# Sparse attention and a feed-forward block in one kernel: leftover blocks of two heads in one slot, another order for the first batch, and the last output tile in two halves

## The chip, the cores and the metric

One Trainium2 chip, of which one core is used. The metric is the time of one execution on the device in microseconds. One more execution was recorded by the hardware profiler; durations and positions below are from that one.

## The reference

Attention over 8 batches, 8 heads, 576 positions and a head dimension of 64, in float32. Heads 0 to 3 see the 32 latest positions ("local"), heads 4 to 7 all earlier positions of the same class modulo 32 ("strided"). The result goes through a feed-forward block with a piecewise gate.

```python
scores = scale * np.matmul(q, k.transpose(0, 1, 3, 2))
mask_local = (rel >= 0) & (rel < stride)
mask_strided = (rel >= 0) & (pos[None, :] % stride == pos[:, None] % stride)
...
attn = np.exp(scores)
attn = attn / (np.sum(attn, axis=-1, keepdims=True) + 1e-09)
...
h = x @ w_in                       # 4608 x 512 by 512 x 2048
g = np.where(pos, h, np.where(neg, 0.0, (h + beta) ** 2 / (4.0 * beta)))
return (g @ w_out).astype(np.float32)
```

## The kernel before

**Attention.** Only blocks that the masks leave are computed: a local head has 18 blocks of 32 queries by 64 keys, a strided head (its positions sorted by class) 11 blocks of 54 by 54. A batch is worked on in four units (`UNITS`): unit 0 has local blocks 0 to 11, unit 1 local blocks 12 to 17, unit 2 strided blocks 0 to 5, unit 3 strided blocks 6 to 10. Two heads make a pair `p`, and `j` is the head within the pair, on partitions 64 j and up. Blocks are stacked on the 128 partitions of a slot: four local ones (`IL`) or two strided ones (`IS`). A unit has `n` slots for each `j`; unit 1 needs 1.5 of them and has 2, unit 3 needs 2.5 and has 3. In `score` (L255) the empty part of the last slot is filled by computing blocks of the same unit a second time (L266).

The steps of a unit, with the letters of the `steps` table (L402): `s` scores on TensorE; `m` mask, a minimum with a mask tile on VectorE out of PSUM, for strided units after a small memset on GpSimd (L291, L297); `x` row maximum on VectorE (L302); `a` subtraction on GpSimd (L306); `e` exponential on ScalarE (L310); `q` row sum on VectorE (L314); `p` plus epsilon on ScalarE (L318); `r` reciprocal on VectorE and product on GpSimd (L322, L323; `w` does the product on VectorE); `f` a transpose of each slot on TensorE (L337); `c` or `d` copies the transposes out of PSUM on ScalarE or VectorE (L349); `v` probabilities times values on TensorE (L368); `h` and `l` write the result as a high and a low float32r part, on ScalarE and VectorE (L395, L399), to the ring `xT`. All float32 matmuls of `s` and `v` appear as two records each in the trace.

**Feed-forward.** The 4608 rows go in 9 chunks `c` of 512, and the 2048 columns of `w_in` in 16 units `f` of 128. For each (c, f): `up` has 12 matmuls of 128x128 by 128x512 (four cuts of the depth by three products of high and low parts, L429) into one of two PSUM buffers "h"; `gate` (L432) has two ScalarE instructions and three on VectorE and ScalarE, the last of which (L446, `gl`) frees that PSUM buffer; `down` (L449), two units later, has 12 matmuls again (L454). Buffer "h" of unit f is that of unit f-2, so `up(0, 2)` waits for `gl` of unit 0. In the last unit `down` copies each of four tiles to one of three SBUF buffers `ob` on ScalarE and stores it by SyncE's queue (L457 to L459).

**Weights.** `w` holds, for each f, a half i=0 (of `w_in`) and a half i=1 (of `w_out`) as raw 64-bit numbers. A half is loaded by SyncE (512 KB) and converted in five steps: `conv_a` on ScalarE, an instruction for the high words (L163) and one for the low words (L166); `conv_b` on VectorE (L171); `conv_c` on GpSimd (L176); `conv_d` on ScalarE (L182); `conv_e` on VectorE (L186). During chunk 0 the halves listed in `halves[f]` are converted in step f: `start_w` issues a, b, c ahead of the gate, `end_w` issues d, e behind it. So in step 0 come halves (0, 1) and (2, 0), in step 1 halves (1, 1) and (3, 0), and so on. Halves (0, 0) and (1, 0) are converted ahead of the loop.

**Order.** The order of instructions on each engine is the order of the program (`manual_schedule`, L478). Ahead of the loop, batch 0 goes through all its steps in an order written out by hand (L491 to L514), among `warm` matmuls on zeros and the conversions of (0, 0) and (1, 0). `up(0, 0)` is split in two calls: the first takes cuts 0 and 1 of the depth (the local heads), the second cuts 2 and 3 (the strided heads) and the products with the low part of the weights. Batches 1 to 7 are spread over the steps f of the loop (`STEPS`, L521): of its four strings the first stands right behind `up`, the second behind `start_w`, the third inside the gate, the fourth behind it. Loads of batch 0, of the first halves and of the queries and keys of batch 1 stand in one row on SyncE (L479 to L490).

## Time and profile before

| | us |
|---|---|
| median of 3 runs (lowest, highest) | 914.03 (913.59, 914.49) |
| the profiled execution's own time | 914.18 |
| span of its profile | 912.4 |

| engine | busy in the span, us |
|---|---|
| TensorE | 899.4 |
| its weight loads (beside the matmuls) | 720.9 |
| ScalarE | 414.4 |
| VectorE | 364.1 |
| GpSimd | 123.1 |

How to read it: PE is TensorE, PEld its weight loads, ACT ScalarE, DVE VectorE, POOL GpSimd, SPq SyncE's queue of transfers. L429 is line 429 of the kernel. A row of the timeline has start, duration, engine, line, operation, tile written <- tiles read, shape, how many in a row, and in brackets the idle time of the engine before it with what ended it. Starts are in microseconds from the start of the span. 914.18 is 1.8 us more than the span; this part lies outside the profile.

### The profile page before, as it was taken

To read this page: it belongs to the slowest core of one execution; us is meant where nothing else is said; L and a number is where in the kernel's file an instruction comes from. 1 tells how busy PE (TensorE), PEld (TensorE's weight loads), DVE (VectorE), ACT (ScalarE), POOL (GpSimd) and SP (SyncE) were. 2 spreads that over 40 slices of the span, in tenths; PEclk is the share of its full clock that TensorE was granted. 3 is DMA by queue.
4 is the path that set the end of the run, shared out by engine and by line. 5 is a ranking of instruction groups with operands and counts; after the bars stand their busy time and mean duration, and the time that the engine had idled before them with its cause. 6 is when DMAs were issued, how large, how long until landed. Compare 5 with 4: busy or idle time off the path is not lost.

```text
span 912.4 us, 17478 instructions
## 1 busy us (share of the span) xinstructions
PE 899.4 (99%) x7550; PEld 720.9 (79%) x7551; DVE 364.1 (40%) x611; ACT 414.4 (45%) x754; POOL 123.1 (13%) x137
## 2 busy tenths in 40 slices
PE   7899999999999999999999999999999999999998
PEld 4688878888788878887888878887888888888886
DVE  6999753423443234323433243334342322222221
ACT  4989744343444444443544344344434343334333
POOL 7464311100211011100210021101110000000000
PEclk9999999999999999999999999999999999999999
DMA  9919131200212021210221021211110010001001
GB/s 353 399 44 311 33 116 62 97 27 10 101 51 70 18 91 47 68 36 1 102 87 33 18 102 36 68 35 42 63 48 1 1 47 1 1 0 47 1 1 46
DMA packets 20381, 61.88 MB, mean 68 GB/s; under 512 B 2256, under 2 KB 2256, under 8 KB 20304
## 3 DMA queue, kind: packets, MB, share of 16 engines
q1 hardware_dynamic: 20304, 60.76, 18.8%
q8 instruction: 59, 0.97, 0.4%
q14 instruction: 18, 0.15, 0.0%
HBM read 51.31 MB, written 9.44 MB: 67 GB/s over the span
## 4 chain that ended last, share of the span: by engine, by line
PE 95%; DMA 2%; DVE 1%; ACT 0%; issue 0%; POOL 0%; SPq 0%; ACTq 0%; DVEq 0%
PE o L454 45%; PE h L429 42%; PE xp L368 3%; PE sc L271 3%; PE tp L337 2%; DMA qk<-in_qk_l 2%; DMA out<-ob 1%; DVE pr L297 0%; DVE st L302 0%; ACT ob L458 0%; DVE st L314 0%; POOL pr L323 0%; DVE w L186 0%; DVE raw L171 0%; DVE h L441 0%
## 5 line engine op out<-in xcount | busy, mean ns | idle before, releaser
L429 PE MATMUL h<-xTh,w 128*128 128x512 f32 x1152 | 381.1, 392 | 1.6 <-DVE gl L446 1.0
L454 PE MATMUL o<-w,gh 128*128 128x512 f32 x1152 | 370.6, 403 | 0.4 <-ACT ob L458 0.4
L429 PEld LDWEIGHTS h<-xTh,w 128*128 128x128 f32 x1152 | 216.3, 188 | 50.8 <-ACT raw L163 1.4
L454 PEld LDWEIGHTS o<-w,gh 128*128 128x128 f32 x1152 | 209.8, 188 | 48.5 <-ACT ob L458 1.8
L438 ACT ACTIVATE u<-h,half 128x512 f32<-128x512 f32 x144 | 99.0, 688 | 315.7 <-PE h L429 313.1
L454 PE MATMUL o<-w,gl 128*128 128x512 f32 x576 | 227.7, 395 | 0.0
L429 PE MATMUL h<-xTl,w 128*128 128x512 f32 x576 | 225.5, 391 | 0.4 <-DVE xTl L399 0.4
L441 DVE SCALAR_TENSOR_TENSOR h<-h,u 128x512 f32<-128x512 f32 x144 | 100.2, 696 | 242.6 <-ACT u L439 242.6
L446 DVE TENSOR_TENSOR gl<-h,gh 128x512 fp32r<-128x512 f32 x144 | 99.5, 691 | 84.5 <-ACT gh L443 77.6
L443 ACT CAST gh<-h 128x512 fp32r<-128x512 f32 x128 | 75.1, 587 | 122.3 <-DVE h L441 122.0
L454 PEld LDWEIGHTS o<-w,gl 128*128 128x128 f32 x576 | 108.3, 188 | 26.0
L429 PEld LDWEIGHTS h<-xTl,w 128*128 128x128 f32 x576 | 108.2, 188 | 25.5 <-DVE xTl L399 1.0
L439 ACT ACTIVATE u<-u 128x512 f32<-128x512 f32 x144 | 91.0, 632 | 4.6
L306 POOL TENSOR_TENSOR pr<-pr,st 128x648 f32<-128x648 f32 (+2 forms) x32 | 40.5, 1268 | 366.5 <-DVE st L302 339.5
L399 DVE TENSOR_TENSOR xTl<-xp,xTh 128x192 fp32r<-128x192 f32 (+7 forms) x74 | 34.8, 522 | 95.3 <-ACT xTh L395 95.3
L323 POOL TENSOR_TENSOR pr<-pr,st 128x648 f32<-128x648 f32 (+2 forms) x32 | 40.5, 1268 | 148.1 <-DVE st L322 141.9
L176 POOL TENSOR_TENSOR raw<-raw 128x512 uint32<-128x512 uint32 (+1 forms) x34 | 34.8, 1037 | 38.8 <-DVE raw L171 13.0
L314 DVE TENSOR_REDUCE st<-pr 128x12 f32<-128x648 f32 (+2 forms) x32 | 26.2, 818 | 33.9 <-ACT pr L310 33.9
L271 PEld LDWEIGHTS sc<-qk 64*32 64x32 f32 (+1 forms) x2048 | 26.6, 116 | 14.5 <-issue 7.8
L368 PEld LDWEIGHTS xp<-pT,v 64*64 64x64 f32 (+2 forms) x1760 | 28.6, 135 | 10.7 <-issue 8.8
L271 PE MATMUL sc<-qk 64*32 64x64 f32 (+1 forms) x2048 | 31.4, 224 | 3.2 <-DMA qk<-in_qk_l 1.4
L368 PE MATMUL xp<-pT,v 64*64 64x32 f32 (+2 forms) x1760 | 32.2, 221 | 0.5 <-ACT pT L349 0.4
(39 smaller groups left out, 351.4 us busy)
## 6 DMA issues: line engine op xcount, KB each, us to landing
raw<-in_w SPq DMA_DIRECT2D x30, 512.0 KB, 9.7
qk<-in_qk_s SPq DMA_DIRECT2D x16, 604.0 KB, 5.7
qk<-in_qk_l SPq DMA_DIRECT2D x16, 576.0 KB, 4.6
out<-ob SPq DMA_DIRECT2D x36, 256.0 KB, 3.5
v<-in_v_l SPq DMA_DIRECT2D x21, 384.0 KB, 3.2
v<-in_v_s SPq DMA_DIRECT2D x7, 384.0 KB, 3.9
v<-in_v_s SPq DMA_DIRECT2D x8, 320.0 KB, 3.1
raw<-in_w SPq DMA_DIRECT2D x4, 256.0 KB, 8.3
```

Source lines behind the costliest of these rows:

```text
L176: nc.gpsimd.tensor_tensor(out=H_, in0=H_, in1=L, op=ALU.add)
L271: nc.tensor.matmul(sc[j][i * Q:(i + 1) * Q, s, p], qk[:, 0, q0:q0 + Q], qk[:, 1, k0:k0 + W], start=True, stop=True)
L306: nc.gpsimd.tensor_tensor(out=pr, in0=pr, in1=st[:, 0].unsqueeze(2).broadcast_to(list(pr.shape)), op=ALU.add)
L323: eng.tensor_tensor(out=pr, in0=pr, in1=st[:, 2].unsqueeze(2).broadcast_to(list(pr.shape)), op=ALU.mult)
L368: nc.tensor.matmul(xp[p][j * D:(j + 1) * D, at:at + R], loaded[b, local, b0 + n][half_, j], pT[half_, j, s, i * Q:i * Q + R], start=True, ...
L429: nc.tensor.matmul(o_ps[c, f], wt[f][:, x, 0, cc * P:(cc + 1) * P], xT[y][:, cc, r0:r0 + CH], start=first and n == 0, stop=last and n == l ...
L438: nc.scalar.activation(u, hp, AF.Relu, bias=half, scale=0.5)
L439: nc.scalar.activation(u, u, AF.Square)
L441: nc.vector.scalar_tensor_tensor(out=hp, in0=hp, scalar=1.0, in1=u, op0=ALU.max, op1=ALU.min)
L443: nc.scalar.copy(gh, hp)
L446: nc.vector.tensor_tensor(out=gl, in0=hp, in1=gh.bitcast(F32), op=ALU.subtract)
L454: nc.tensor.matmul(o_ps[c][t], gs[x][:, t * P:(t + 1) * P], wt[f][:, y, 1, :], start=f == 0 and n == 0, stop=f == NF - 1 and n == 2)
```

## The change

Three edits, and one small one.

1. `slots(u)` gives the number of slots for each `j`: (3, 3), (2, 1), (3, 3), (3, 2). `seat` puts the leftover blocks of j=1 behind those of j=0 in the last slot of j=0: on partitions 64 and up, where a second copy of blocks stood before. `score` runs over blocks and computes each once. `mask` treats full slots on 128 partitions and the shared slot in two instructions of 64 partitions. All that follows has fewer slots: 6 instead of 8 groups in unit 1, 10 instead of 12 in unit 3.
2. The first batch is written as one string for a new helper `begin`. Half (2, 0) is converted in it (A20, L20, B20, C20, D20, E20), and `halves` has it no more. The product of unit 1 goes to VectorE (w1 in place of r1), its copy to VectorE (d1) and that of unit 3 to ScalarE (c3). The first part of `up(0, 0)` (U0) stands ahead of v3, the second (U1) behind l3. There are 8 and 9 warm matmuls in place of 7 and 8.
3. The last output tile is copied in two halves, by VectorE and ScalarE, into a tile of the pool "s" in place of "ob", and stored by two transfers.
4. `h3 l3` of a batch moves from inside the gate to behind it (step 14 of `STEPS`).

The renaming that follows from 1 (`probs` and `flipped` no longer carry `n`) is left out below.

```diff
+    def slots(u):
+        n, rest = divmod(UNITS[u][2], IL if UNITS[u][0] else IS)
+        return n + (rest > 0), n
+
+    def seat(u, n, j):
+        I = IL if UNITS[u][0] else IS
+        s, i = divmod(n, I)
+        return (j, s, i) if s < UNITS[u][2] // I else (0, s, i + j * I // 2)
...
         def score(u, pairs=range(2)):
...
             for p in pairs:
-                for s in range(n):
-                    for i in range(I):
-                        blk = b0 + (s * I + i if s * I + i < nb else s * I + i % (nb - s * I))
...
+                for n in range(nb):
+                    q0 = (b0 + n) * (QL if local else WS)
+                    k0 = max(q0 - ST, 0) if local else q0
+                    for j in range(2):
+                        _, s, i = seat(u, n, j)
+                        qk = loaded[b, p0 + p, "qk"][j * D:(j + 1) * D]
+                        nc.tensor.matmul(sc[j][i * Q:(i + 1) * Q, s, p], qk[:, 0, q0:q0 + Q],
+                                         qk[:, 1, k0:k0 + W], start=True, stop=True)
...
         def mask(u):
...
-            for j in range(2):
-                o = pr[:, j * n * 2:(j + 1) * n * 2].rearrange("p (n h) w -> p n h w", h=2)
-                nc.vector.tensor_tensor(out=o, in0=sc[j], in1=m, op=ALU.min)
+            todo = [(j, slice(0, P), 0, ns[1], j * ns[0]) for j in range(2)]
+            if ns[0] > ns[1]:
+                todo += [(j, slice(j * 64, j * 64 + 64), ns[1], ns[0], ns[1]) for j in range(2)]
+            for j, part, s0, s1, at in todo:
...
+                nc.vector.tensor_tensor(out=o, in0=sc[j][part, s0:s1], in1=m.broadcast_to([o.shape[0], n, 2, W]), op=ALU.min)
...
         def flip(u):
...
-            for j in range(2):
+            for j, n in enumerate(slots(u)):
                 tp = psum(kinds(u, "F", j), [P, n, P], f"tp_{b}_{u}_{j}")
...
         def down(c, f, gs):
...
-                ob = o_p.tile([P, DM], F32, tag="ob", name=f"ob_{c}_{t}")
-                nc.scalar.copy(ob, o_ps[c][t])
-                nc.sync.dma_start(out[c * CH + t * P:c * CH + (t + 1) * P, :], ob)
+                e0 = 0 if (c, t) < (NCH - 1, CH // P - 1) else DM // 2
+                if e0:
+                    last = s_p.tile([P, DM], F32, tag="s", name="ob_last")
+                    nc.vector.tensor_copy(last[:, :e0], o_ps[c][t][:, :e0])
+                    nc.sync.dma_start(out[NT - P:, :e0], last[:, :e0])
+                ob = last[:, e0:] if e0 else o_p.tile([P, DM], F32, tag="ob", name=f"ob_{c}_{t}")
+                nc.scalar.copy(ob, o_ps[c][t][:, e0:])
+                nc.sync.dma_start(out[c * CH + t * P:c * CH + (t + 1) * P, e0:], ob)
...
-    for g in range(2, NF):
+    for g in range(3, NF):
         halves[g - 2].append((g, 0))
+
+    def begin(names):
+        conv = {"A": lambda f, i: conv_a(f, i, (False,)), "L": lambda f, i: conv_a(f, i, (True,)),
+                "B": conv_b, "C": conv_c, "D": conv_d, "E": conv_e}
+        for name in names.split():
+            if name[0] == "U":
+                up(0, 0, name == "U0", name == "U1")
+            elif name[0] == "W":
+                warm("o", int(name[1:]))
+            elif name[0] in conv:
+                conv[name[0]](int(name[1]), int(name[2]))
+            else:
+                first(name)
...
-        warm("o", 7)
-        first("s0 s1 s2 s3")
-        warm("o", 8)
-        first("m0 x0 a0 m1 x1 a1 e0 m2 x2 a2 e1")
-        conv_a(0, 0, (False,))
-        first("q0 p0")
-        conv_a(0, 0, (True,))
-        first("e2 r0 m3 x3 a3 q1 p1 r1 f0 c0 e3 q2 p2")
-        conv_b(0, 0)
-        first("r2")
-        conv_a(1, 0)
-        first("v0 f1 q3 p3 r3")
-        conv_c(0, 0)
-        first("f2 h0 c1 d2 l0 v1 f3 h1 d3 l1 v2")
-        conv_b(1, 0)
-        conv_d(0, 0)
-        conv_c(1, 0)
-        first("h2 v3")
-        conv_e(0, 0)
-        first("l2 h3 l3")
-        up(0, 0, last=False)
-        up(0, 0, first=False)
-        conv_d(1, 0)
-        conv_e(1, 0)
+        begin("""
+            W8 s0 m0 x0 s1 m1 s2 s3 m2 x1 a0 x2 e0 L00 q0 a1 a2 e1 q1 p0 p1 A00 r0 m3 x3 W9 e2 a3 L10 q2 f0
+            w1 c0 p2 r2 e3 B00 q3 A10 v0 f1 p3 L20 h0 f2 r3 d1 A20 d2 v1 f3 C00 h1 D00 c3 v2 l0 l1 B20 U0
+            B10 h2 C10 v3 h3 C20 D10 E00 l2 l3 D20 U1 E20 E10
+        """)
...
-                 14: ("v3", "", "h3 l3", "")}
+                 14: ("v3", "", "", "h3 l3")}
```

## The prediction

> **What bounds the kernel now.** I first read the busy time by stretches (columns: stretch, its length, busy time and count of PE, PEld, DVE, ACT, POOL, then granted clock, DMA share, GB/s):

> ```profile
> 0.00:24.36 24.36, 18.10 (x525) 11.85 (x526) 15.49 (x32) 10.87 (x24) 16.78 (x35) 0.93 0.94 357
> 24.36:35.99 11.63, 9.62 (x43) 6.37 (x37) 9.67 (x16) 10.98 (x20) 4.96 (x5) 1.00 1.02 407
> 35.99:130.00 94.01, 94.01 (x959) 75.85 (x959) 78.08 (x135) 74.82 (x141) 39.91 (x40) 1.00 0.42 151
> 130.00:880.00 750.00, 749.63 (x5913) 604.42 (x5913) 254.60 (x421) 307.46 (x555) 61.45 (x59) 1.00 0.13 44
> 880.00:908.05 28.05, 28.05 (x122) 22.44 (x120) 6.25 (x9) 9.67 (x16) 0.00 (x0) 1.00 0.03 9
> 908.05:912.40 4.35, 0.00 (x1) 0.00 (x0) 0.00 (x0) 0.58 (x1) 0.00 (x0) 0.99 0.50 188
> ```

> From 35.99 to 908.05 PE is busy all but 0.37 us, at full clock. Any matmul that leaves this stretch shortens the run by its own time, any work on other engines costs nothing while they keep up. Three places are left: PE's own work in the middle, the way to 35.99, and the 4.35 us behind the last matmul. The edits touch all three.

> **PE's work in the middle (edit 1).** Rows of batch 1, whose steps run between FFN matmuls:

> ```profile
> 35.99 1.17 PE L271 MATMUL sc<-qk 64*32 64x64 f32 x96
> 42.81 0.86 PE L271 MATMUL sc<-qk 64*32 64x64 f32 x64
> 54.81 0.82 PE L337 MATMUL tp<-ident,pr 128*128 128x128 f32 x6
> 61.11 0.92 PE L271 MATMUL sc<-qk 64*64 64x54 f32 x48
> 74.89 0.60 PE L337 MATMUL tp<-ident,pr 128*128 128x128 f32 x4
> ```

> Unit 1 has 8 blocks times 2 pairs times 2 heads before, 6 after: 8 matmuls or 16 records fewer. A record costs (1.17 - 0.86) / 32 = 0.0097 us, so 0.155 us. Unit 3 goes from 48 to 40 records. Its row has 0.92 us; with the fixed part of unit 0's row (1.17 - 96 x 0.0097 = 0.24) a record costs (0.92 - 0.24) / 48 = 0.0142, so 0.11 us. A transpose costs (0.82 - 0.60) / 2 = 0.11, and units 1 and 3 lose one each: 0.22 us. Together 0.49 us a batch, in 7 batches under the FFN **3.4 us**. Bounds: if the doubled blocks ran wholly in the shadow of the others, only the transposes count, 7 x 0.22 = 1.5; the upper end is 3.7 with 0.0192 (0.92 / 48) for each of unit 3's records, 7 x (0.155 + 0.154 + 0.22).

> The mask pays in instructions: two of unit 1 become four.

> ```profile
> L297 DVE TENSOR_TENSOR pr<-sc,m_loc 128x384 f32<-128x384 f32 x16 | 8.2, 552 | 24.0 <-PE sc L271 24.0
> L297 DVE TENSOR_TENSOR pr<-sc,m_loc 128x256 f32<-128x256 f32 x16 | 6.0, 419 | 6.0 <-PE sc L271 6.0
> L302 DVE TENSOR_REDUCE st<-pr 128x12 f32<-128x768 f32 x8 | 7.6, 953 | 0.3
> L302 DVE TENSOR_REDUCE st<-pr 128x8 f32<-128x512 f32 x8 | 5.5, 687 | 0.3
> ```

> 133 ns go with 128 elements, so one of 128 takes 0.29 and four 1.14 against 0.84: 0.3 us more on DVE. Taking 64 partitions like 128 is my choice, no row shows it; at half price the sum is 0.84 again. The row maximum falls from 512 to 384 elements, by 0.13, and the sum likewise: DVE stands even, ACT and POOL gain. In chunk 0 DVE is busy 78.08 of 94.01 us; there the conversion of (2, 0) is gone as well. At no cost, then; without that cover 0.3 us would stand behind each gate.

> **The way to 35.99 (edit 2).** PE, ACT and DVE in the first batch:

> ```profile
> 15.15 0.87 PE L337 MATMUL tp<-ident,pr 128*128 128x128 f32 x6 [0.21 <-POOL pr L323]
> 16.41 1.98 PE L368 MATMUL xp<-pT,v 64*64 64x32 f32 x96 [0.39 <-ACT pT L349]
> 19.34 0.87 PE L337 MATMUL tp<-ident,pr 128*128 128x128 f32 x6 [0.37 <-POOL pr L323]
> 23.52 0.33 PE L368 MATMUL xp<-pT,v_None 54*64 54x54 f32 x7 [0.83 <-issue]
> 25.74 0.51 PE L429 MATMUL h<-xTh,w 128*128 128x512 f32 x1 [0.18 <-ACT xTh L395]
> 26.66 0.50 PE L429 MATMUL h<-xTl,w 128*128 128x512 f32 x1 [0.42 <-DVE xTl L399]
> 32.39 0.47 PE L429 MATMUL h<-xTh,w 128*128 128x512 f32 x1 [1.00 <-DVE gl L446]
> 33.50 0.73 PE L429 MATMUL h<-xTh,w 128*128 128x512 f32 x2 [0.41 <-DVE w L186]
> 37.09 0.73 PE L454 MATMUL o<-w,gh 128*128 128x512 f32 x2
> ```
> ```profile
> 23.87 2.27 ACT L395 CAST xTh<-xp 128x324 fp32r<-128x324 f32 x4 [1.64 <-PE xp L368]
> 28.73 0.67 ACT L438 ACTIVATE u<-h,half 128x512 f32<-128x512 f32 x1
> ```
> ```profile
> 24.65 2.50 DVE L399 TENSOR_TENSOR xTl<-xp,xTh 128x324 fp32r<-128x324 f32 x4 [0.39 <-ACT xTh L395]
> 31.55 0.69 DVE L446 TENSOR_TENSOR gl<-h,gh 128x512 fp32r<-128x512 f32 x1
> 32.16 1.28 DVE L186 TENSOR_TENSOR w<-raw,w 128x512 fp32r<-128x512 f32 x2
> ```

> I walked the new string queue by queue with these durations (those of smaller tiles scaled as above). (a) Up to f0 nothing is won: q0 stands behind as much DVE work, f0 comes at 15.15 again, and the ninth warm matmul lies ahead of it. (b) c0 now stands behind e2 and the low words of (1, 0) on ACT, and v0 starts about 0.4 later, its bulk near 17.2. (c) From there PE runs f1, f2, v1, f3, v2 in one row, for their inputs come from DVE (r1's product, d1) in time: 1.5 + 0.4 + 0.6 + 0.9 + 0.6 + 1.0 put v2's end at 22.2, against 23.85 (23.52 + 0.33), where PE had waited for POOL (0.37) and for its own instructions (0.83). (d) h2 and h3 on ACT follow c3, and h3 waits for v3, which stands behind U0: end 25.1, against 26.14. l3 ends at 25.9 against 27.15, U1 at 27.2 against 28.6. (e) Behind it ACT has D20 and the two instructions for (0, 1), but not the two for (2, 0): the gate of unit 0 runs at 27.2 in place of 28.73 and `gl` ends at 30.75 in place of 32.24. up(0, 1) is through by then, so up(0, 2) still waits, 0.9 of the 1.00 us; the 0.41 us for the weights of unit 2 is gone, for E20 is done at 26.8. up(0, 2) then ends at 33.6 against 36.0. (f) s0 of batch 1 comes next, and needs its queries and keys:

> ```profile
> L222 SPq DMA_DIRECT2D qk<-in_qk_l x4: 328/400/431, 0.7 to 23.2; - x4
> DMA to landing us min/median/max: 4.1/5.8/10.9
> ```

> The second pair is issued at 23.2 and lands 10.9 later, 34.1. The loads ahead of it keep all DMA engines busy and are not touched, so this stays. The second half of s0 (0.55) ends at 34.6 at the earliest, and the first `down` can start 37.09 - 34.6 = **2.5 us** earlier at most. The same walk over the old order gave 36.8 for 37.09, 0.3 too early; I take **2.2 us**. Low end: a pause for instructions of 0.83 ahead of v2 again, and a POOL product that stops a DVE conversion (0.5), leave 0.9.

> Does the gain last through chunk 0? Unit 5's w_in is ready at 50.27 and PE wants it at 52.21:

> ```profile
> 48.99 1.28 DVE L186 TENSOR_TENSOR w<-raw,w 128x512 fp32r<-128x512 f32 x2
> 52.21 2.76 PE h L429 x12
> ```

> 1.9 us of lead. PE moves by 2.2 and ACT, DVE by 1.5 (e), so 0.7 is used up and 1.2 left. Edit 4 (h3, l3 behind the gate) lies beside down(0, 12), up(0, 15) and down(0, 13), three stretches of 2.8 us before anything reads it: at nothing; without these it would cost l3's 1.2 us once.

> The clock speaks against (c):

> ```profile
> 7.80:11.20 3.40, 1.78 (x93) 1.56 (x95) 3.33 (x7) 0.41 (x1) 1.92 (x2) 1.00 0.99 340
> 11.20:14.60 3.40, 3.18 (x26) 1.27 (x19) 3.05 (x7) 3.02 (x6) 2.94 (x4) 0.50 1.02 405
> 14.60:18.00 3.40, 2.72 (x94) 2.04 (x92) 3.13 (x7) 2.22 (x7) 2.91 (x4) 1.00 1.01 398
> ```

> After 1.78 busy us in 3.40 the granted clock fell to 0.50, after 2.72 it stayed. With v0 later the new stretch has 0.4 of warm matmuls, 0.87 of f0 and 0.85 of v0, 2.1 us: between both. If it falls, the 3 us of PE work from 18.0 on take till 23.9 and (c)'s gain is lost. [...]

> **The end (edit 3).**

> ```profile
> 907.66 0.39 PE L454 MATMUL o<-w,gl 128*128 128x512 f32 x1
> 908.75 0.58 ACT L458 COPY ob<-o 128x512 f32<-128x512 f32 x1 [0.77 <-DMA out<-ob]
> 906.61 3.09 SPq L459 DMA_DIRECT2D out<-ob  x4
> DMA to landing us min/median/max: 2.0/2.0/2.1
> ```

> The last matmul ends at 908.05, the copy starts at 908.75, held by the store of the first tile, whose buffer it shares; its store is issued at 909.37 (906.61 + 3.09 - 0.33) and lands at 911.4, the span ends 1.0 later. After: both halves start at 908.1 and take 0.42 (L297's 256 elements); the issues follow at 908.55 and 908.9, for one takes SyncE 0.33. Landing 2.0 behind the second: 910.9, **0.5 us** won. Low end 0.3, if half a tile from PSUM takes 0.58; upper end 0.8, if 128 KB land sooner by their share of bytes, 0.3 (256 KB at 400 GB/s are 0.64).

> **The sum.** 3.4 + 2.2 + 0.5 = 6.1. The profiled execution took 914.18: 914.18 - 6.1 = 908.1. It stood 0.15 over the median of 914.03, so I say **908.0**; below, the same base.

> **The rivals.**

> *The first batch gives back most of its gain*, by the clock or the pause for instructions ahead of v2: 0.9 in place of 2.2, **909.2**. For it the two rows of pauses and the 2.1 us; against it that fewer score instructions move the pause behind v2.

> *ACT and DVE do not follow PE in chunk 0*: weights of some unit 3 to 7 come late, and PE waits where it was ahead. The first batch then yields nothing: 914.0 - 3.9 = **910.1**. For it 78.08 and 74.82 busy of 94.01, against it the 1.2 us left.

> *The doubled blocks were free* (the change does not do what it says): 1.5 in place of 3.4, **909.8**. Against it the difference between 96 and 64 records.

> *Slower:* the leftovers of the two heads now sit on different rows and different columns of the array; if such a matmul runs alone, at a mean of 0.22 us a record in place of 0.01, the 24 records left of the last slots (16 in unit 1, 8 in unit 3) cost 5 us a batch, 7 x 5 - 6 = 29 us, **943**. It decides from (6.0 / 7) / 24 = 0.036 us a record on. Against it: unit 3's and the value matmuls change rows and columns from one to the next, at 0.014.

> **Chances.** Forecast 0.55, with its own range 907.0 to 908.8 from the terms' ends; first batch 0.22; chunk 0 0.06; free blocks 0.06; several of these together, 911 to 914, 0.06; slower 0.05. The range, 906.8 to 910.2, holds the first four. 0.2%, 1.8 us, is about what a measurement of this kernel can tell from no change: faster than 912.2 is 0.91, within 0.04, slower 0.05.

> **What would show it.** Right: s0 of batch 1 in rows of 96, 48, 48, 40 records and 10 transposes a batch; the first `down` at about 34.9; no wait named for the weights of unit 2; PE without a gap from there to about 902.5; the last store issued at 0.9 behind the last matmul. Wrong: a granted clock of 0.50 between 18 and 22; a wait for weights or `gl` in chunk 0; score rows that do not get shorter.

## The result: 0.16% slower, and the profile after

| | before | after |
|---|---|---|
| median, us (lowest to highest; 12 runs each) | 914.29 (913.25 to 916.05) | 915.75 (913.35 to 917.76) |
| the profiled execution | 914.18 | 914.58 |
| its span | 912.41 | 912.80 |
| first `up` starts | 24.36 | 27.83 |
| first `down` starts | 37.09 | 41.20 |
| last matmul ends | 908.05 | 909.07 |
| from first `down` to last matmul | 870.97 | 867.87 |
| behind the last matmul | 4.36 | 3.73 |

The ratio of the times is 1.0016, with a 95% interval of 1.0008 to 1.0024. The forecast of 908.0 us and its range were wrong. The two traces divide the difference: the start lost 4.11 us, the middle won 3.10, the end 0.63, in sum 0.4 us more. The medians differ by 1.46 us. The twelve executions of after spread with their granted clock (mean of the span), from 0.996 at 913.35 us to 0.988 at 917.76 us; only one of them has a trace, so where the slower ones lose the rest is not shown.

The start in the timeline of TensorE after (start, duration, engine, line, tiles, count, and the idle time ahead with what ended it):

```profile
12.73 0.60 PE L483 MATMUL warm_o<-zeros 128*128 128x512 bf16 x2
15.08 0.87 PE L350 MATMUL tp<-ident,pr 128*128 128x128 f32 x6 [1.76 <-POOL pr L336]
16.73 1.97 PE L381 MATMUL xp<-pT,v 64*64 64x32 f32 x95 [0.77 <-ACT pT L362]
21.63 0.19 PE L381 MATMUL xp<-pT,v 64*64 64x32 f32 x1 [2.94 <-issue]
21.75 1.99 PE L350 MATMUL tp<-ident,pr 128*128 128x128 f32 x9
27.83 0.80 PE L442 MATMUL h<-xTh,w 128*128 128x512 f32 x1
29.40 0.79 PE L381 MATMUL xp<-pT,v 54*64 54x54 f32 x40
...
41.20 0.73 PE L467 MATMUL o<-w,gh 128*128 128x512 f32 x2
```

f0 comes as forecast, at 15.08, and the bulk of v0 at 16.73, half a us ahead of the forecast. Then TensorE stops one matmul ahead of the end of v0 for 2.94 us. "issue" says that the profile shows no other engine and no load that it waited for. Before, the only such row behind f0 was the 0.83 us in v2. What follows runs at a granted clock of 0.50, as five stretches show (columns as in the prediction):

```profile
11.76:15.17 3.41, 1.65 (x9) 0.58 (x7) 3.34 (x10) 2.61 (x6) 3.26 (x4) 1.00 1.00 403
15.17:18.59 3.42, 2.57 (x101) 2.22 (x102) 2.83 (x7) 2.75 (x7) 2.18 (x2) 1.00 1.04 419
18.59:22.00 3.41, 0.47 (x9) 0.26 (x3) 0.22 (x1) 1.28 (x4) 2.33 (x3) 1.00 0.96 380
22.00:25.40 3.40, 3.40 (x59) 3.01 (x58) 2.67 (x6) 1.10 (x3) 0.00 (x0) 0.50 1.03 411
25.40:28.82 3.42, 3.42 (x55) 2.83 (x54) 1.99 (x6) 2.45 (x7) 1.89 (x2) 0.50 1.03 410
```

The pause leaves 0.47 busy us in 3.41, and for 6.82 us from 22.00 on the granted clock is 0.50. From f1 to the start of v3 TensorE takes 7.65 us here (21.75 to 29.40), and 4.77 us for the same rows at full clock in run e11 below (19.19 to 23.96): 2.9 us lost. Pause and clock together, 5.8, would put the first `down` at 42.9 with nothing won; it is at 41.20, so some 1.7 us were won around them (0.8 of it is before's own pause in v2).

The middle: batch 1's rows that answer to 64 and 48 score records and to 4 and 6 transposes, and the end:

```profile
46.93 0.77 PE L280 MATMUL sc<-qk 64*32 64x64 f32 x48
78.90 0.49 PE L350 MATMUL tp<-ident,pr 128*128 128x128 f32 x3
84.86 0.92 PE L280 MATMUL sc<-qk 64*64 64x54 f32 x40
110.74 0.71 PE L350 MATMUL tp<-ident,pr 128*128 128x128 f32 x5
```
```profile
41.20:130.00 88.80, 88.80 (x827) 71.41 (x820) 73.95 (x133) 72.65 (x138) 37.56 (x38) 1.00 0.39 136
130.00:880.00 750.00, 750.00 (x5779) 604.73 (x5769) 257.12 (x449) 305.27 (x556) 58.34 (x60) 1.00 0.13 44
880.00:909.07 29.07, 29.07 (x126) 23.26 (x124) 6.93 (x10) 9.98 (x16) 0.00 (x0) 1.00 0.02 9
```
```profile
909.18 0.42 DVE L473 COPY ob_last<-o 128x256 f32<-128x256 f32 x1 [4.97 <-PE o L467]
909.63 0.33 SPq L474 DMA_DIRECT2D out<-ob_last  x1
909.63 0.37 ACT L476 COPY ob_last<-o 128x256 f32<-128x256 f32 x1 [0.64 <-DVE ob_last L473]
910.05 0.41 SPq L477 DMA_DIRECT2D out<-ob_last  x1
```

The local row got shorter (0.77 for 0.86), the strided one with 40 records did not (0.92 as with 48), and TensorE is busy without a gap from 41.20 to the end. The two halves of the last tile did not run side by side: ScalarE waited for VectorE's half.

**Where the pause may come from.** The page lists a queue that moves instructions during the run. First the lines of before, then those of after:

```profile
PE 899.4 (99%) x7550; PEld 720.9 (79%) x7551; DVE 364.1 (40%) x611; ACT 414.4 (45%) x754; POOL 123.1 (13%) x137
...
q8 instruction: 59, 0.97, 0.4%
```
```profile
PE 898.2 (98%) x7345; PEld 720.7 (79%) x7345; DVE 363.6 (40%) x645; ACT 411.6 (45%) x754; POOL 116.3 (13%) x136
...
q8 instruction: 58, 0.95, 0.4%
```

Matmuls and weight loads are 15,101 instructions before and 14,690 after: 256 and 253 to a packet of 16.4 KB (59 and 58 packets, 0.97 and 0.95 MB). That TensorE's instructions come in blocks of 256, one to a packet, is my estimate from these counts; no row names the engine that a packet is for. Counted along the trace, with TensorE's semaphore instructions and within two (some records are missing), all pauses over 0.25 us that are put down to "issue" lie where such blocks would end, 256 apart: at instruction 450, 706 or 962, in every kernel of this study. After's 2.94 us is at 706. The queue's line for a stretch shows whether a packet of q8 falls into it: before it did between 14 and 17, after not there but between 18.5 and 20.7:

```profile
q8 instruction: 1, 0.02, 2.0%
```
```profile
q8 instruction: 1, 0.02, 5.1%
```

My reading of the packets that start between 10 and 30 us (start to end), with the count of TensorE instructions that stand ahead of f0, and the longest pause for "issue" behind f0:

```
                 ahead of f0   packets                                    pause (count, from, to)
before               544   14.59-15.54  20.93-21.90  27.25-28.33    962  22.68-23.52
after                500   18.80-20.59  25.57-26.64                 706  18.69-21.63
```

**Theory F** (fetch): TensorE asks for the next block when the reading of its program gets to some instruction between 500 and 544 (an estimate from the two rows above; no trace shows the asking). Before, that instruction lay among the last scores and the warm matmuls, ahead of the waits of f0 and v0. Edit 1 takes 48 score instructions out of the first batch and one warm matmul more in each of the two rows adds 4, so it would now lie behind these waits, and the block comes 4.2 us later (18.80 for 14.59). Rivals: **C**, the clock is the cause and the pause a by-product (more warm matmuls help by their busy time); **L**, low words of (1, 0) stand ahead of c0 on ScalarE, wait for a load, and hold up TensorE; and that the new order itself is worse.

### The profile page after: what moved, and what is told of

Same layout as the page of the kernel before. It is cut to its first block, busy times and chain, and to the rows that moved or that the text cites. A ratio compares the mean times of both kernels' runs of the same rounds, so it can differ in the third digit from the quotient of the medians.

```text
span 912.8 us, 17125 instructions
## 1 busy us (share of the span) xinstructions
PE 898.2 (98%) x7345; PEld 720.7 (79%) x7345; DVE 363.6 (40%) x645; ACT 411.6 (45%) x754; POOL 116.3 (13%) x136
## 4 chain that ended last, share of the span: by engine, by line
PE 97%; DMA 1%; ACT 0%; issue 0%; DVE 0%; SPq 0%; DVEq 0%
PE o L467 45%; PE h L442 43%; PE xp L381 4%; PE sc L280 3%; PE tp L350 2%; DMA raw<-in_w 1%; DMA qk<-in_qk_l 1%; SPq L247 0%; ACT pT L362 0%; DVE h L454 0%; DVE gl L459 0%; DVE gh L458 0%; ACT u L451 0%; ACT raw L178 0%; DVE xTl L412 0%
## 5 line engine op out<-in xcount | busy, mean ns | idle before, releaser
L454 DVE SCALAR_TENSOR_TENSOR h<-h,u 128x512 f32<-128x512 f32 x144 | 100.4, 697 | 277.4 <-ACT u L452 277.0
L459 DVE TENSOR_TENSOR gl<-h,gh 128x512 fp32r<-128x512 f32 x144 | 99.6, 692 | 85.0 <-ACT gh L456 78.3
L319 POOL TENSOR_TENSOR pr<-pr,st 128x768 f32<-128x768 f32 (+3 forms) x32 | 37.4, 1169 | 370.5 <-DVE st L315 365.8
L412 DVE TENSOR_TENSOR xTl<-xp,xTh 128x192 fp32r<-128x192 f32 (+7 forms) x74 | 34.9, 521 | 68.1 <-ACT xTh L408 68.1
L336 POOL TENSOR_TENSOR pr<-pr,st 128x768 f32<-128x768 f32 (+3 forms) x31 | 36.7, 1183 | 144.5 <-DVE st L335 136.2
L381 PEld LDWEIGHTS xp<-pT,v 64*64 64x64 f32 (+2 forms) x1760 | 28.6, 134 | 11.4 <-issue 9.2
L280 PEld LDWEIGHTS sc<-qk 64*32 64x32 f32 (+1 forms) x1856 | 25.9, 116 | 13.8 <-issue 7.3
L327 DVE TENSOR_REDUCE st<-pr 128x12 f32<-128x768 f32 (+3 forms) x32 | 24.2, 759 | 25.8 <-ACT pr L323 25.8
L408 ACT CAST xTh<-xp 128x192 fp32r<-128x192 f32 (+7 forms) x74 | 30.9, 512 | 6.4 <-PE xp L381 6.3
```

The lines of the kernel that those rows point to most:

```text
L280: nc.tensor.matmul(sc[j][i * Q:(i + 1) * Q, s, p], qk[:, 0, q0:q0 + Q], qk[:, 1, k0:k0 + W], start=True, stop=True)
L319: nc.gpsimd.tensor_tensor(out=pr, in0=pr, in1=st[:, 0].unsqueeze(2).broadcast_to(list(pr.shape)), op=ALU.add)
L336: eng.tensor_tensor(out=pr, in0=pr, in1=st[:, 2].unsqueeze(2).broadcast_to(list(pr.shape)), op=ALU.mult)
L381: nc.tensor.matmul(xp[p][j * D:(j + 1) * D, at:at + R], loaded[b, local, b0 + n][half_, j], pT[half_, h, s, i * Q:i * Q + R], start=True, ...
L412: nc.vector.tensor_tensor(out=dst[1], in0=src, in1=dst[0].bitcast(F32), op=ALU.subtract)
L454: nc.vector.scalar_tensor_tensor(out=hp, in0=hp, scalar=1.0, in1=u, op0=ALU.max, op1=ALU.min)
```

## The experiments

The count ahead of f0 is moved by small warm matmuls (two instructions each, 24 of them 0.75 us). Ratios are to the kernel before, run on the same chip beside it.

**The count alone.** After, with 24 or 8 small matmuls (548 or 516 ahead of f0):

```diff
-    def warm(kind, n):
+    def warm(kind, n, small=0):
...
+        for _ in range(small):
+            nc.tensor.matmul(t[:, :32], zeros, zeros[:, :1].broadcast_to([P, 32]), start=True, stop=True)
...
-                warm("o", int(name[1:]))
+                warm("o", int(name[1:]), 24 if name == "W9" else 0)
```

> The changed kernel with 24 small matmuls on zeros (128x32, 48 PE instructions with their weight loads) behind the nine warm ones, so that 548 in place of 500 PE instructions lie ahead of the first transposes. Theory F (fetch): PE's instructions come in blocks of 256, and the block that begins at its instruction 706 is asked for when PE gets to an instruction between 514 and 544. In the changed kernel that point lies behind the waits of the first transposes and the first value matmuls. Here it lies ahead of them again: the fetch starts at 13 to 15 us instead of 18.8, the pause of 2.94 us in the value matmuls of unit 0 is gone, the clock stays at 1.00 behind 15 us, the first down starts near 35.5 instead of 41.2, and the time is 908 to 910. Theory O (order): the hand-written order itself leaves PE idle and the clock falls; nothing changes, 914 to 916. Theory D (chance of the DMA queues): the fetch is late whatever the count; 914 to 916.

912.14 us (911.00 to 914.21), ratio 0.9976 [0.9964, 0.9988]. Instructions added, time gone: the block comes at 14.40 to 15.40 and the pause at 706 is not there any more. But F's 908 to 910 was not reached, the first `down` starts at 38.55, and another wait stands in the pause's place:

```profile
17.14 0.65 ACT L178 ACTIVATE raw<-raw 128x512 uint32<-128x512 uint32 x1 [1.94 <-DMA raw<-in_w]
```
```profile
18.21 2.10 PE L381 MATMUL xp<-pT,v 64*64 64x32 f32 x96 [1.82 <-ACT pT L362]
```

That is L10 on ScalarE, and c0 behind it: v0's bulk at 18.21 and not 16.7. L is real too, but comes second.

> As the former with 8 small matmuls, 516 PE instructions ahead of the first transposes. F: where the asking instruction is after 516, pause and time are those of the changed kernel (914 to 916); where it lies at 515 or 516, it is as with 24 (908 to 910). O and D: 914 to 916.

915.35 us (913.78 to 917.88), ratio 1.0011 [1.0000, 1.0021]: as slow as after. The block comes at 18.98, and the pause is the same one, 9 matmuls ahead of v0's end for 1:

```profile
21.50 0.44 PE L381 MATMUL xp<-pT,v 64*64 64x32 f32 x9 [2.96 <-issue]
```

The warm matmuls end later here (this execution has a half clock from 10.67 to 14.08) and TensorE idles less ahead of f0 (0.17 for 1.76 us), so by C it should have helped. It is a step between 516 and 544 instructions, not a slope.

**The parts alone.** Edit 1 on the kernel before (496 ahead of f0), and the new order with four blocks a slot as before (548):

```diff
 # slots only: before, with slots(u), seat(u, n, j), score, mask and flip of after
 # order only: before, with begin("W8 s0 m0 ... E20 E10") and halves from g = 3 on of after
```

> The kernel before with the shared slots alone (old order of the first batch, old end): 496 PE instructions ahead of the first transposes instead of 544. F: a pause at instruction 706 in the value matmuls of unit 0 or right behind, half clock after it, first down later than 37.1 by 1 to 4 us; the 2.1 us of the middle (0.30 in each of 7 batches, as the changed kernel shows it) are lost again, 913 to 916. O: no pause, since the order is the old one: 914.1 - 2.1 = 912.0 or less.

915.93 us (914.94 to 917.32), ratio 1.0016 [1.0006, 1.0025]. The slots alone, in the order of before, lose as much as the whole change. The block comes at 19.07 and TensorE stops behind v0:

```profile
21.53 1.86 PE L350 MATMUL tp<-ident,pr 128*128 128x128 f32 x8 [2.78 <-issue]
```

The middle, 867.95 us, has the whole gain of after. So the edit that takes work away brings the loss, by its count.

> The kernel before with the new order of the first batch alone (blocks doubled as before): 548 PE instructions ahead of the first transposes. F: fetch at 13 to 15 us, no pause of more than 1 us ahead of the second value matmuls, first down at 35 to 36, time 914.1 - 1.5 = 912.6 or somewhat less. O: pause and half clock as in the changed kernel, first down near 41, time 917 to 918.

915.61 us (913.50 to 916.56), ratio 1.0012 [1.0002, 1.0022]; the profiled execution was the lowest. In it the block comes at 14.30 and nothing stops at 706, as F has it, but the first `down` starts at 36.85, only 0.24 earlier than before and later than the 35 to 36 expected. TensorE runs ahead of before and loses it at 962:

```profile
21.55 0.80 PE L368 MATMUL xp<-pT,v_None 54*64 54x54 f32 x38
23.63 0.38 PE L368 MATMUL xp<-pT,v_None 54*64 54x54 f32 x10 [1.28 <-issue]
```

Before, this pause ended at 23.52. Why the median lies above before's is open: the higher runs have no trace here.

**L, with the count mended.** The low words move behind c0 and h0:

```diff
-  ... e2 a3 L10 q2 f0 w1 c0 p2 r2 e3 B00 q3 A10 v0 f1 p3 L20 h0 ...
+  ... e2 a3 q2 f0 w1 c0 p2 r2 e3 L10 B00 q3 A10 v0 f1 p3 h0 L20 ...
```

> The changed kernel with the 24 small matmuls, and with the low words of halves (1, 0) and (2, 0) converted behind the steps c0 and h0 of the string instead of ahead of them. Theory L (loads): ScalarE works in order, so c0 and h0 wait behind these two for the landing of their halves (15.6 to 17.1 and 18.7 to 20.2 us). Then c0 starts 0.7 us behind the first transposes, the bulk of v0 at 16.9 to 17.1 instead of 18.2, and the first down 1 to 1.5 us earlier than with the 24 small ones alone: 910.3 to 911.3. Rival: unit 0's values wait for something else, and nothing changes against 24 small ones alone, 912.1.

911.32 us (910.44 to 912.21), ratio 0.9961 [0.9945, 0.9977]; v0's bulk starts at 16.46 for 18.21, the first `down` at 37.82 for 38.55. The interval overlaps that of e1_small24; it is the trace that shows L.

> The changed kernel with the two moves of the former alone, 500 PE instructions ahead of the first transposes. Theory F: the pause at instruction 706 stays, and with it the half clock: 914 to 916. Theory L alone: 1 us less than the changed kernel, with no pause.

The move without small matmuls (500 ahead of f0): 916.13 us (913.34 to 917.93), ratio 1.0013 [1.0001, 1.0025], with the block at 18.70 and a pause of 1.67 us up to 21.29. L costs something only where F doesn't.

> The two moves, six warm matmuls in place of nine and 60 small ones behind them: 566 + 48 = 614 PE instructions ahead of the first transposes. F: the block from 962 on begins at a place that is 72 instructions earlier in the program than with 24 small ones, in the transposes of unit 3, and is asked for around the end of unit 0's values; pauses there of 0.6 us or less, first down at 35.5 to 36.5, 909.5 to 911. Rival: the count matters only for the block at 706, and the time is that of the kernel with 24 small ones and the moves.

The move with W6 and 60 small ones (614 ahead): 912.26 us (910.24 to 915.84), ratio 0.9973 [0.9960, 0.9985]; the block at 14.61, and only 0.29 us idle at 962. The time missed the 909.5 to 911 expected: the clock is at half from 17.23 to 20.64, and the first `down` starts at 37.08.

**The clock.** e5 still had a half clock from 16.35 on. Thirteen warm matmuls in place of nine should close the hole ahead of f0:

> The changed kernel with the 24 small matmuls, the two moves and 13 warm matmuls in place of 9 ahead of the first transposes. Theory C (clock): half clock behind 16 us follows a window of 3.41 us with about 2 us of PE work or less (1.85 with 9 warm ones); here the window has 0.85 more, the clock stays, and the first down comes at 36.3 to 37.0 instead of 37.8; where the window of the warm ones itself is at half clock they end 0.8 us later than the product of unit 0 and cost that. Median 910.3 to 911.3, against 911.3 with 9. Rival: the clock has little to do with the first down, and nothing changes by over 0.3 us in it.

A miss: 913.01 us (910.94 to 914.73), ratio 0.9982 [0.9973, 0.9991], no better than e5. The clock holds through v0 as meant, TensorE is ahead, stops at 961, and the clock falls behind that:

```profile
23.62 0.44 PE L381 MATMUL xp<-pT,v_None 54*64 54x54 f32 x12 [1.93 <-issue]
```
```profile
21.50:24.91 3.41, 1.48 (x28) 1.04 (x19) 1.56 (x5) 1.58 (x5) 2.36 (x2) 1.00 1.02 408
24.91:28.32 3.41, 2.74 (x44) 1.91 (x43) 2.42 (x4) 2.20 (x5) 0.00 (x0) 0.50 1.03 407
```

**The halves at the end.** After, with the last tile copied whole by ScalarE into its own buffer and stored by one transfer:

```diff
                 e0 = 0 if (c, t) < (NCH - 1, CH // P - 1) else DM // 2
-                if e0:
-                    ...
+                ob = s_p.tile([P, DM], F32, tag="s", name="ob_last") if e0 else o_p.tile(...)
+                nc.scalar.copy(ob, o_ps[c][t])
+                nc.sync.dma_start(out[c * CH + t * P:c * CH + (t + 1) * P, :], ob)
```

> The changed kernel with its last tile copied whole by ScalarE into the buffer of its own, and stored by one transfer. In the changed kernel's profile ScalarE's half waited until VectorE's half was done, so the halves may bring nothing: from the end of the last matmul to the end of the span 3.6 to 3.8 us, as with halves (3.7; before 4.35). If the halves do bring something: 4.0 or more.

One execution, 917.53 us, in which the half clock lasted from 21.52 to 38.58, so its time says nothing of the end. Its trace does:

```profile
912.00 0.58 ACT L472 COPY ob_last<-o 128x512 f32<-128x512 f32 x1
912.61 0.33 SPq L473 DMA_DIRECT2D out<-ob_last  x1
```

The copy starts with the last matmul's end (911.96) and 3.71 us lie behind that, against 3.73 with halves. Two later runs with the whole tile, e10 and e12, have 3.71 and 3.70. The own buffer is the gain, the halves are none.

**The old order with the rest of the change.** e2, 24 small matmuls behind the eight warm ones (544 ahead of f0), the last tile whole in its own buffer:

> The kernel before with the shared slots, its old order of the first batch with 24 small matmuls behind its eight warm ones (544 PE instructions ahead of the first transposes, as before), and the last tile copied whole into a buffer of its own. F: no pause at instruction 706, first down at 37.0 to 37.6 as before, 867.9 us from there to the last matmul, 3.7 behind it: 914.1 - 3.0 - 0.6 = 910.5, 910.3 to 911.3. So the new order of the first batch is worth nothing measurable. If the new order is worth what the prediction gave it, this kernel is 2 us slower than the one with 24 small matmuls and the two moves (913.3).

912.12 us (910.96 to 914.19), ratio 0.9972 [0.9960, 0.9983]. That is a little above the 910.3 to 911.3 expected, and its interval overlaps that of e5: with the queues as they are, the new order adds nothing that can be told. It stops at the same place as e9, here with

```profile
23.47 0.33 PE L381 MATMUL xp<-pT,v_None 54*64 54x54 f32 x6 [1.19 <-issue]
```

In before, e4, e9 and e10 this row starts at 23.52, 23.63, 23.62 and 23.47, whether TensorE got to it at 21.7 (e9) or at 22.7 (before). So the block that begins there has a time of its own. Its packets start at 20.9 to 21.2, 6.3 to 6.9 us behind the ones before, while the loads keep the DMA engines busy (a DMA share of 1.01 to 1.03 in these four runs). (In e1_small24 and e5, where c0 or the clock held TensorE up, they start at 22.87 and 21.99.) Two readings: a fixed pace, or a queue behind the loads.

**Loads held back.** e9, with half (0, 1), the halves up to unit 5 and the queries and keys of batch 1 issued behind h1, and not ahead of the string:

```diff
-        stage(6)
-        for p in range(2):
-            load_qk(1, p)
...
+    def rest():
+        nonlocal staged
+        load_w(0, 1, loaded[0, 1, "qk"][0:1, 0, 0:1])
+        staged = 1
+        for p in range(2):
+            load_qk(1, p)
+        stage(6)
...
-  ... C00 h1 D00 c3 v2 ...
+  ... C00 h1 S D00 c3 v2 ...    # S: rest()
```

> The kernel with 13 warm and 24 small matmuls and the two moves, and all weight loads behind half (2, 0) held back until ScalarE has copied the high part of unit 1 (about 21.3 us), with the queries and keys of batch 1 second among them. In all kernels with 544 or more instructions ahead of the first transposes the pause at instruction 962 ended at 23.5 to 23.6, however early PE got there. Theory Q (full queues): the fetch takes its 3 us from asking because all DMA engines are busy with the loads. Here they are idle from 19 to 21.5; the fetch for 962 starts within 1 us of 20 us and the pause ends by 22.4; the first down comes at 36.5 to 37.5 with a steady clock against 38.9. Theory R (rate): blocks come every 6.3 us whatever else the DMA engines do; the pause ends at 23.5 as before, and the first down is at 38 or later.

910.78 us (910.14 to 911.52), ratio 0.9954 [0.9937, 0.9970], the best of all, and clear of e9; against e5 the intervals overlap. TensorE, and its stretches:

```profile
17.29 1.98 PE L381 MATMUL xp<-pT,v 64*64 64x32 f32 x96 [0.24 <-ACT pT L362]
19.19 1.20 PE L350 MATMUL tp<-ident,pr 128*128 128x128 f32 x9
20.32 1.03 PE L381 MATMUL xp<-pT,v_None 64*64 64x32 f32 x48
21.29 0.77 PE L350 MATMUL tp<-ident,pr 128*128 128x128 f32 x5
21.98 0.92 PE L381 MATMUL xp<-pT,v_None 54*64 54x54 f32 x48
22.84 0.50 PE L442 MATMUL h<-xTh,w 128*128 128x512 f32 x1
...
23.96 0.79 PE L381 MATMUL xp<-pT,v 54*64 54x54 f32 x40
...
35.85 0.73 PE L467 MATMUL o<-w,gh 128*128 128x512 f32 x2
```
```profile
17.50:20.90 3.40, 3.32 (x136) 3.03 (x137) 2.56 (x8) 3.40 (x10) 2.39 (x3) 1.00 0.09 35
20.90:24.30 3.40, 3.40 (x108) 2.68 (x104) 3.40 (x9) 3.40 (x9) 1.73 (x3) 1.00 0.33 95
```

With the DMA engines at 0.09 and 0.33 the blocks come at 19.75 and 23.68, 3.9 us apart, and no pause is left. v0, f1 to v2 run in one row at full clock, and the first `down` starts 3.1 us earlier than in e9 (38.93). In these runs, then, full queues and not a fixed pace: 3.9 us from one to the next at these shares, 6.3 to 6.9 at 1.01 to 1.03. The 3 us from asking in Theory Q are an estimate, for no trace shows the asking. Some of the 3.1 us is given back in the middle (868.94, against 868.53 in e9 and 867.87 in after), where weight loads of `up` now wait for a conversion:

```profile
PEld h L442 <- DVE w L198: 1.2, 2, 0.8
```

**The same loads held back in the old order** (e10 with `rest()` behind h1):

> e10 with the same loads held back as in e11 (half (0, 1), the halves up to unit 5 and the queries and keys of batch 1, issued behind h1), in the order of before. It tells whether the new order is worth anything once PE's instructions come in time. If the order is what counts then (my prediction's steps (c) to (e), about 1 to 2 us): no pause at 962, but PE still waits for POOL's products, for gl and 0.3 to 0.4 us for unit 2's weights, first down between 36.6 and 37.5, against 35.85 in e11; the time 911.4 to 912.5. If late instruction blocks were the whole of the loss and the order is worth nothing: first down between 35.5 and 36.2, the time within 0.4 us of e11, 910.8.

912.99 us (910.41 to 914.56), ratio 0.9981 [0.9970, 0.9991], 2.2 us above e11, a little outside both expectations. Again no pause at 962: v2 runs whole to 22.4. Then the old order pays: ScalarE has the conversions of (0, 1) and (2, 0) ahead of the gate, and (0, 1) now lands late.

```profile
26.76 0.66 ACT L175 ACTIVATE raw<-raw 128x512 f32<-128x512 f32 x1 [1.19 <-DMA raw<-in_w]
```
```profile
32.71 0.76 PE L442 MATMUL h<-xTh,w 128*128 128x512 f32 x1 [2.15 <-ACT raw L178]
```
```profile
29.09:32.51 3.42, 1.47 (x7) 0.89 (x5) 2.35 (x5) 3.39 (x7) 1.08 (x2) 1.00 0.99 368
32.51:35.93 3.42, 3.22 (x7) 2.22 (x8) 2.02 (x5) 2.58 (x6) 1.70 (x2) 0.50 1.03 422
```

up(0, 2) starts 0.9 us later than in e11 (31.82), TensorE idles for 2.15, and the clock falls once more: the first `down` at 38.39. Of the 2.5 us between the two first `down`s 0.45 stand already at the first `up` (23.28 against 22.84). The rest comes with the late load and the clock behind it, which hit the old order harder; so the new order does better with these loads held back, but what the order alone is worth is not shown. The two ran on different chips, and the intervals of their ratios touch.

## Why the prediction was wrong, point by point

**The step that failed** is the first batch, (a) to (c): "From there PE runs f1, f2, v1, f3, v2 in one row, for their inputs come from DVE ... in time." I walked five queues and left out a sixth supply, the instructions (59 packets on q8 in before). The one trace of it, the 0.83 us in v2, I took for something that follows the count, and dismissed it because "fewer score instructions move the pause behind v2". The runs show the other sign: with a lower count the packet came late, at 18.70 to 19.07 (after, e1_small8, e2, e6) for 14.30 to 14.61 (before, e1_small24, e4, e7). 496 to 516 ahead of f0 gave a pause of 1.7 to 3.1 us at 706 (after, e1_small8, e2, e6, e8), 544 and more gave none there (before, e1_small24, e4, e5, e7, e9, e10, e11, e12). The rival "the first batch gives back" named the pause and the clock, but ahead of v2 and at 1.3 us; it was the pause at the end of v0 with a fallen clock behind it, 5.8 us.

**And with the count mended, (c) still fails.** In e4, e9 and e10 TensorE is early and waits for the next block until 23.5 or 23.6, as before. (c) holds only in e11, where the loads are held back: v2 ends at 22.9, against 22.2 forecast.

**(a), (b)** held as to f0 (15.08 for 15.15). v0's bulk at 16.73 was earlier than the 17.2 forecast: that execution's load of (1, 0) landed at 15.62. In e1_small24 it landed at 17.12, and v0 came at 18.21. Step (b) had put c0 behind the low words, but not behind their load. The 0.5 us of the low end, a conversion on VectorE beside a product on GpSimd, is the difference of two rows of before: L171 took 0.97 us from 16.84 on, with the product busy from 16.47 to 17.51, and 0.42 from 23.25 on, with GpSimd idle.

**(e)** held in part: the 0.41 us for unit 2's weights is gone in after and e4, and up(0, 2) waits about 1.0 us for `gl`, as I said (0.9).

**The clock.** I feared the stretch 14.6 to 18.0 with 2.1 busy us. It held 2.57 in after's windows and the clock stayed at 1.00; it fell to 0.50 one window later, behind the one with the pause, of 0.47 busy us in 3.41. The clock also fell behind 1.47 (e12), 1.48 (e9) and, in before, 1.78.

**Edit 1** looks the right size, 3.10 us for 3.4, in part by luck. By the rows a local unit won 0.09 a batch for 0.155, the strided scores nothing for 0.11, the two transposes 0.22 as forecast, together 0.31 a batch or 2.2 in seven. Some 0.4 of the 3.10 is a wait that this execution of before had and after had not,

```profile
542.42 0.73 PE L454 MATMUL o<-w,gh 128*128 128x512 f32 x2 [0.37 <-ACT ob L458]
```

e4, which has the doubled blocks and no such wait, takes 870.53 us in the middle, and e2, with edit 1 alone, 867.95, so edit 1 is worth about 2.6 us; some 0.4 of that are smaller differences that I can't place. Why 40 strided records cost as much as 48 is open. The prediction's sign of "10 transposes a batch" was a miscount: after has 6, 3, 6 and 5, which is 20, and before 22. The slower rival, leftovers that run alone, fell: 48 records take 0.77 us. Its 0.22 us a record is the mean of one in before (L271, 222 and 225 ns).

**Edit 3** was mis-sized by little (0.63 for 0.5) and wrong in its mechanism: the halves run one behind the other, and the gain is the buffer (e8). **Edit 4** and the cover of VectorE and ScalarE in chunk 0 held: TensorE is busy 88.80 of 88.80 us from 41.20 on.

## What to carry to other kernels

Treat TensorE's instructions as a load of their own: where a row of it waits for "issue", count matmuls, weight loads and semaphore instructions up to it, and see whether the counts lie 256 apart, as 450, 706 and 962 did here. An edit that takes small matmuls away ahead of a wait can make the next packet late: 18.80 in after, 19.07 with edit 1 alone (e2), for 14.59 in before. Some cheap matmuls put back brought it to 14.40 (e1_small24). Fewer transfers in the queues at that time made the block after it come sooner, 3.9 us behind the one before for 6.3 to 6.9 (e11); by themselves, without the count mended, they were not tried. And when a pause ends at the same time however early the engine comes, see to its supply first: TensorE 1 us earlier at the pause of 962 (21.7 in e9 for 22.7 in before) got on at 23.62 for 23.52, and e11, with count and queues mended, takes 910.78 us against 915.75.
